# First batch of a spectral FFN kernel: biases added by VectorE while t1 leaves PSUM, and the threshold's last subtraction on GpSimd

## The chip, the core and the metric

The kernel runs on one core of one Trainium2 chip. The metric is the device time of one execution in microseconds (us), the median of the runs shown. A core has five engines that run side by side, each through its own list of instructions in a fixed order: TensorE (PE, with its weight loads PEld), VectorE (DVE), ScalarE (ACT), GpSimd (POOL) and SyncE (SP), which here issues all DMA transfers.

## The reference

A spectral layer (a transform along the sequence, a complex linear layer with biases, a soft threshold, the inverse transform) is followed by a feed-forward layer on every token. Here B = 8, S = 3008, D = 256, FF = 2048.

```python
X = np.fft.rfft(x, axis=1)
Xr, Xi = X.real, X.imag
Yr = Xr @ w_r - Xi @ w_i + b_r
Yi = Xr @ w_i + Xi @ w_r + b_i
Yr = np.sign(Yr) * np.maximum(np.abs(Yr) - 0.01, 0.0)
Yi = np.sign(Yi) * np.maximum(np.abs(Yi) - 0.01, 0.0)
y = np.fft.irfft(Yr + 1j * Yi, n=S, axis=1)
h = y.reshape(B * S, D) @ w_in
out = (h - np.tanh(h)) @ w_out
```

## The kernel before

The 8 batches go through the spectral layer one after the other, and their tokens in 48 chunks through the feed-forward layer. The spectral work of batches 1 to 7 is woven into the feed-forward work of the batch before. Batch 0 has nothing to be woven into: it runs first, by itself, and that is where the change lies. The order of the instructions on every engine is that in which the code issues them (a manual schedule); nothing reorders them later, and an instruction that waits holds up everything behind it on its engine.

Batch 0 is cut into 12 units (`WholeSpectrum(0, jp)`, called unit 0 to 11 below). The main loop runs i = 0 to 11, and pass i holds a different step of several units:

- PE: the transform of unit i into a PSUM bank (`dft`, L532); the products of unit i-1 (`cross`): a bias product of a matrix of ones with the row of biases (L551), the two cross terms into the same bank `vv` and the shared term `t1` into the bank with the tag `o0` (L557). In passes 4, 6, 8 and 10 the inverse transforms of units i-4 and i-3 follow (L612).
- ACT: copies t1 of unit i-2 out of PSUM (`common`, L573, tile `tb`), copies the transform of unit i to `xf` (L537), then for unit i-2 the two halves of the soft threshold, `up` = relu(y - 0.01) and `mn` = relu(-y - 0.01) (L586, L590), and the copies of the inverse (L623).
- DVE: adds tb and vv of unit i-2 to `y` (`blend`, L579), the sum `sf` of unit i (L542), a share of the unpacking of feed-forward weights, and last `join` of unit i-2: mn = up - mn (L603).
- The weights come as 64-bit floats and are unpacked in blocks b0, b1, ... of 128x512 numbers. A block takes five DVE steps, called e (L221), m (L236), f (L239), s (L242) and v (L245) here; two steps on ACT between e and f (L225, L232); and a rounding on ACT (L249) with the remainder on POOL (L250). In passes 2 to 4 one of three matrices of the linear layer is split as well: ACT rounds (L142), POOL, DVE, POOL subtract (L143). Table `on_dve` sets which block steps stand in which pass; in pass 8 they are f, s, v of b3 and e of b4, in pass 9 m, f, s, v of b4 and e of b5, in pass 10 m, f, s, v of b5 and e, m of b6.

`o0` is one single bank: t1 of the next unit can be written only when t1 of the last one has been read. `tb` has the tag `xi` with two buffers before. After the loop units 8 to 11 finish in code written out by hand (units 10 and 11 threshold on DVE alone, L594 and L595), batch 1's first transforms begin (L291, PE), and then the feed-forward layer.

The biases come to SBUF by one transfer before: `bias_rows`, 33 partitions. A tile `bias` on 128 partitions is loaded later for the other batches (their biases in another order of columns).

Of the kernel before, what the change touches and what calls it, by code (L numbers as in the profile page):

```python
# [92 lines left out]


@with_exitstack
def spectral_ffn(ctx, tc, x, w_r, w_i, w_in, w_out, x_fold, b_turned, f1, f1b, f1f, f2, f2f, i1, i1w, i2, out):
    nc = tc.nc
    P = 128
    w_in, w_out = w_in.bitcast(U32), w_out.bitcast(U32)
# [55 lines left out]
    def load_linear():  # L155
        wr = ffn.tile([P, 2, D], F32, name="wr_f", tag="g_h")
        wi = ffn.tile([P, 2, D], F32, name="wi_f", tag="g_l")
        nc.sync.dma_start(out=wr, in_=w_r.rearrange("(t p) e -> p t e", p=P))
        nc.sync.dma_start(out=wi, in_=w_i.rearrange("(t p) e -> p t e", p=P))
        rows = load_bias(work.tile([33, 2, D], F32, name="bias_rows", tag="tmp", bufs=4), 33)  # L160
        return wr, wi, rows

    def load_bias(dst, n):
        both = b_turned.rearrange("(o k) d -> o (k d)", o=1).to_broadcast([n, 2 * D])
        nc.sync.dma_start(out=dst.rearrange("p k d -> p (k d)"), in_=both)
        return dst

    def combine_linear(wr, wi, rows, zero):
# [4 lines left out]
        ones = work.tile([P, P], F32R, name="ones", tag="s_l")  # L173
        nc.vector.tensor_scalar(out=ones, in0=zero[:, :P], scalar1=1.0, scalar2=None, op0=ALU.add)
        top = work.tile([33, 2 * D], F32R, name="bias_top", tag="tmp", bufs=4)
        flat = rows.rearrange("o r e -> o (r e)")
        nc.scalar.copy(out=top, in_=flat)
        brow = work.tile([P, 2 * D], F32R, name="brow", tag="ot", bufs=1)
        nc.vector.tensor_copy(out=brow, in_=zero)
        nc.vector.tensor_copy(out=brow[0:1], in_=top[0:1].bitcast(F32))  # L180
        nc.vector.tensor_tensor(out=brow[32:33], in0=flat[32:33], in1=top[32:33].bitcast(F32), op=ALU.subtract)
        return (wr, w2, w3), (ones, brow)
# [333 lines left out]
    class WholeSpectrum(Spectrum):  # L516
# [27 lines left out]
        def cross(self):  # L544
            if self.jp % 3 < 2:
                self.vv = ps_h.tile([P, 512], F32, name="ps_v", tag="h")
            else:
                self.vv = ps_o.tile([P, 512], F32, name="ps_v", tag="o1")
            ones, brow = bias_rows
            by_part = self.vv.rearrange("p (r i j) -> p r i j", r=2, j=2)  # L550
            nc.tensor.matmul(by_part, ones, brow.rearrange("p (r j i) -> p r i j", r=2, j=2), start=True, stop=False)  # L551
            self.t1 = ps_o.tile([P, 512], F32, name="ps_t1", tag="o0")[:, :D]
            for k, (dst, lhs) in enumerate((
                (self.vv[:, :D], self.xf[:, :, 1]), (self.vv[:, D:], self.xf[:, :, 0]), (self.t1, self.sf),
            )):
                for t in range(2):
                    nc.tensor.matmul(dst, lhs[:, t], whole_lin[2 - k][:, t, :], start=k == 2 and t == 0, stop=k > 0 and t == 1)  # L557

        def cross_apart(self):
            ones, brow = bias_rows  # L560
# [4 lines left out]
            for dst, lhs, w, b in ((self.t1, self.sf, 0, None), (low, self.xf[:, :, 1], 2, 0), (high, self.xf[:, :, 0], 1, D)):  # L565
                if b is not None:
                    nc.tensor.matmul(paired(dst, D), ones, in_turn(brow[:, b:b + D]), start=True, stop=False)
                for t in range(2):
                    nc.tensor.matmul(dst, lhs[:, t], whole_lin[w][:, t, :], start=b is None and t == 0, stop=t == 1)

        def common(self):
            self.tb = work.tile([P, D], F32, name="tb0", tag="xi")
            nc.scalar.copy(out=self.tb, in_=self.t1)  # L573

        def blend(self):
            self.y = self.temp("y", "g")
            if not hasattr(self, "sides"):
                both = self.vv.rearrange("p (r d) -> p r d", r=2)
                nc.vector.tensor_tensor(out=self.y, in0=self.tb.unsqueeze(1).to_broadcast([P, 2, D]), in1=both, op=ALU.add)  # L579
                return  # L580
            for r, side in enumerate(self.sides):
                nc.vector.tensor_tensor(out=self.y[:, r], in0=self.tb, in1=side, op=ALU.add)

        def above(self):
            self.up = self.temp("up", "th")
# [14 lines left out]
            self.below()  # L600

        def join(self):
            nc.vector.tensor_tensor(out=self.mn, in0=self.up, in1=self.mn, op=ALU.subtract)  # L603

        def inverse(self, parts=None, banks=None, first=0):
            banks = banks or [ps_f.tile([P, 512], F32, name="ps_i1", tag="f") for _ in range(2)]
# [159 lines left out]
    with tc.manual_schedule(engines={E.PE, E.Activation, E.DVE, E.Pool, E.SP}):  # L766
# [21 lines left out]
        for i in range(len(steps) + 1):  # L788
            if i < len(steps):
                steps[i][0].whole(steps[i][1])  # L790
            if i >= 1:
# [364 lines left out]
```

## Time and profile before

| what | before |
|---|---|
| median of 3 runs | 2439.88 us (2439.38 to 2440.62) |
| the profiled execution's own time | 2442.07 us |
| span of the profiled execution | 2440.3 us |
| granted TensorE clock over the span | 1.000 |
| PE busy | 2427.9 us (99%) |
| DVE busy | 1781.2 us (73%) |
| ACT busy | 1349.6 us (55%) |
| POOL busy | 34.5 us (1%) |

The span is the time from the first to the last instruction; the profiled execution's own time is 1.8 us longer, and the runs without a profile are 2.2 us below that. The busy shares are means over the whole span: what bounds a stage has to be read in that stage. Batch 0's units lie between 26 and 87 us.

### The profile page before, as it was taken

To read this page: it belongs to the slowest core of one execution; us is meant where nothing else is said; L and a number is where in the kernel's file an instruction comes from. 1 tells how busy PE (TensorE), PEld (TensorE's weight loads), DVE (VectorE), ACT (ScalarE), POOL (GpSimd) and SP (SyncE) were. 2 spreads that over 40 slices of the span, in tenths; PEclk is the share of its full clock that TensorE was granted. 3 is DMA by queue.
4 is the path that set the end of the run, shared out by engine and by line. 5 is a ranking of instruction groups with operands and counts; after the bars stand their busy time and mean duration, and the time that the engine had idled before them with its cause. 6 is when DMAs were issued, how large, how long until landed. Compare 5 with 4: busy or idle time off the path is not lost.

```text
span 2440.3 us, 47561 instructions
## 1 busy us (share of the span) xinstructions
PE 2427.9 (99%) x19274; PEld 2134.1 (87%) x19274; DVE 1781.2 (73%) x3251; ACT 1349.6 (55%) x2781; POOL 34.5 (1%) x31
## 2 busy tenths in 40 slices
PE   9999999999999999999999999999999999999999
PEld 6798888888888898888888889888898989888888
DVE  4887887787777776777767777677776767755555
ACT  5765555555555555555555555555555555555554
POOL 2110000000000000000000000000000000000000
PEclk9999999999999999999999999999999999999999
DMA  8633216322534212332123231332211111111000
GB/s 253 193 102 111 86 65 153 91 74 81 142 88 108 76 54 67 97 98 69 61 72 100 82 94 53 81 82 80 62 61 46 59 58 43 51 34 26 21 9 17
DMA packets 135146, 195.31 MB, mean 80 GB/s; under 512 B 13521, under 2 KB 99631, under 8 KB 134928
## 3 DMA queue, kind: packets, MB, share of 16 engines
q1 hardware_dynamic: 134928, 192.29, 27.3%
q8 instruction: 151, 2.47, 0.4%
q14 instruction: 67, 0.55, 0.1%
HBM read 114.12 MB, written 78.12 MB: 79 GB/s over the span
## 4 chain that ended last, share of the span: by engine, by line
PE 93%; DVE 4%; ACT 1%; DMA 1%; issue 1%; SPq 0%; ACTq 0%; DVEq 0%
PE o L742 39%; PE h L709 38%; PE ps_v L423 4%; PE ps_i L667 3%; PE ps_t L423 2%; PE ps_f L507 2%; PE ps_f L343 1%; DVE g L723 1%; PE ps_i L479 1%; PE ps_i L480 1%; PE ps_i L478 1%; DVE gl L729 1%; PE ps_f L291 1%; DVE w_s L242 0%; DVE w_f L239 0%
## 5 line engine op out<-in xcount | busy, mean ns | idle before, releaser
L726 ACT CAST gh<-g 128x502 fp32r<-128x502 f32 (+2 forms) x768 | 469.0, 611 | 568.4 <-DVE g L723 558.6
L729 DVE TENSOR_TENSOR gl<-g,gh 128x502 fp32r<-128x502 f32 (+2 forms) x768 | 522.2, 680 | 331.9 <-ACT gh L726 322.0
L723 DVE TENSOR_TENSOR g<-h,th 128x502 f32<-128x502 f32 (+2 forms) x768 | 520.4, 678 | 218.7 <-ACT th L720 212.9
L720 ACT ACTIVATE th<-h 128x502 f32<-128x502 f32 (+2 forms) x768 | 454.1, 591 | 379.1 <-PE h L709 375.0
L742 PE MATMUL o<-gh,wout_l 128*128 128x502 f32 (+2 forms) x1536 | 587.2, 382 | 0.2 <-DVE ot L760 0.2
L742 PE MATMUL o<-gh,wout_h 128*128 128x502 f32 (+2 forms) x1536 | 576.5, 375 | 0.0
L742 PE MATMUL o<-gl,wout_h 128*128 128x502 f32 (+2 forms) x1536 | 576.1, 375 | 0.3 <-DVE gl L729 0.3
L709 PE MATMUL h<-yh,win_l 128*128 128x502 f32 (+2 forms) x1536 | 451.9, 376 | 1.4 <-DVE g L723 1.0
L709 PE MATMUL h<-yh,win_h 128*128 128x502 f32 (+2 forms) x1536 | 450.3, 375 | 0.0
L709 PE MATMUL h<-yl,win_h 128*128 128x502 f32 (+2 forms) x1536 | 450.3, 375 | 0.0
L742 PEld LDWEIGHTS o<-gh,wout_l 128*128 128x128 f32 x1536 | 290.2, 189 | 54.2 <-issue 11.7
L709 PEld LDWEIGHTS h<-yh,win_l 128*128 128x128 f32 x1536 | 288.6, 188 | 40.9 <-DVE g L723 4.6
L742 PEld LDWEIGHTS o<-gl,wout_h 128*128 128x128 f32 x1536 | 290.0, 189 | 36.2 <-DVE gl L729 1.1
L709 PEld LDWEIGHTS h<-yl,win_h 128*128 128x128 f32 x1536 | 290.4, 189 | 34.4
L709 PEld LDWEIGHTS h<-yh,win_h 128*128 128x128 f32 x1536 | 290.3, 189 | 34.4
L742 PEld LDWEIGHTS o<-gh,wout_h 128*128 128x128 f32 x1536 | 290.6, 189 | 26.4
L465 DVE TENSOR_TENSOR y<-tb,ps_v 64x256 f32<-64x256 f32 x336 | 140.0, 417 | 3.4
L700 ACT CAST yh<-yt 128x470 fp32r<-128x470 f32 (+38 forms) x200 | 90.0, 483 | 23.7 <-PE h L709 21.3
L701 DVE TENSOR_TENSOR yl<-yt,yh 128x470 fp32r<-128x470 f32 (+38 forms) x200 | 82.3, 430 | 16.6 <-ACT yh L700 15.6
L411 DVE TENSOR_TENSOR xl<-ps_f,xh 128x256 fp32r<-128x256 f32 x168 | 63.6, 419 | 27.5 <-ACT xi L409 26.0
L667 PEld LDWEIGHTS ps_i<-i,zin 48*64 48x64 f32 x4096 | 65.2, 135 | 9.5 <-issue 5.5
L142 ACT CAST z_h<-mn 128x512 fp32r<-128x512 f32 x84 | 52.5, 625 | 36.3 <-DVE mn L456 36.3
(116 smaller groups left out, 2130.4 us busy)
## 6 DMA issues: line engine op xcount, KB each, us to landing
xt<-in_x_fold SPq DMA_DIRECT2D x52, 512.0 KB
at<-a SPq DMA_DIRECT2D x96, 256.0 KB
z<-zo SPq DMA_DIRECT2D x92, 256.0 KB
zin<-z SPq DMA_DIRECT2D x92, 240.0 KB
a<-st SPq DMA_DIRECT2D x216, 96.0 KB
out<-ot SPq DMA_DIRECT2D x29, 502.0 KB
turn_l<-turns SPq DMA_DIRECT2D x72, 128.0 KB
turn_h<-turns SPq DMA_DIRECT2D x72, 128.0 KB
```

Source lines behind the costliest of these rows:

```text
L411: nc.vector.tensor_tensor(out=xl[:, s], in0=whole[s], in1=xh[:, s].bitcast(F32), op=ALU.subtract)
L423: nc.tensor.matmul(paired(dst, D), lhs[:, t], in_turn(rhs[:, t, :]), start=n == 0, stop=n == 5)
L465: nc.vector.tensor_tensor(out=self.y[ri * 64:(ri + 1) * 64, jj, :], in0=self.tb[rows, ri, :], in1=self.side(ri)[rows], op=ALU.add,)
L667: nc.tensor.matmul(pv[h][64 * c:64 * c + 64, t, 47 * k:47 * k + 47], self.zt[rows, k, at:at + 64], i2t[rows, :47], start=True, stop=True,)
L700: nc.scalar.copy(out=yh, in_=y)
L701: nc.vector.tensor_tensor(out=yl, in0=y, in1=yh.bitcast(F32), op=ALU.subtract)
L709: nc.tensor.matmul(paired(h, n), lhs[:, t, f * P:(f + 1) * P], moving(rhs[:, t], n), start=k == 0, stop=k == 5,)
L720: nc.scalar.activation(out=th[:, :n], in_=h[:, :n], func=AF.Tanh)
L723: nc.vector.tensor_tensor(out=g[:, :n], in0=h[:, :n], in1=th[:, :n], op=ALU.subtract)
L726: nc.scalar.copy(out=gh[:, :n], in_=g[:, :n])
L729: nc.vector.tensor_tensor(out=gl[:, :n], in0=g[:, :n], in1=gh[:, :n].bitcast(F32), op=ALU.subtract)
L742: nc.tensor.matmul(paired(self.o[t], n), lhs[:, f, t * P:(t + 1) * P], in_turn(rhs[:, :n]), start=f == 0 and k == 0, stop=f == NF - 1 and ...
```

## The change

For the units of batch 0, the 13 products with ones go away, and so do the tiles `ones`, `bias_top` and `brow` with the five instructions that make them. Instead the tile `bias` is loaded early (128 partitions, plain order of columns), and `common` becomes an instruction of DVE: it reads t1 from PSUM twice over, adds both biases and writes a tile of 128x512. That tile has the tag `ot` with one buffer. `blend` then reads this tile. `join` moves from DVE to POOL. The other order of the biases is loaded into the same tile later, where the load for the other batches stood.

```diff
-        rows = load_bias(work.tile([33, 2, D], F32, name="bias_rows", tag="tmp", bufs=4), 33)
-        return wr, wi, rows
+        return wr, wi
...
-            ones, brow = bias_rows
-            by_part = self.vv.rearrange("p (r i j) -> p r i j", r=2, j=2)
-            nc.tensor.matmul(by_part, ones, brow.rearrange("p (r j i) -> p r i j", r=2, j=2), start=True, stop=False)
             self.t1 = ps_o.tile([P, 512], F32, name="ps_t1", tag="o0")[:, :D]
...
         def common(self):
-            self.tb = work.tile([P, D], F32, name="tb0", tag="xi")
-            nc.scalar.copy(out=self.tb, in_=self.t1)
+            self.tb = work.tile([P, 2, D], F32, name="tb", tag="ot", bufs=1)
+            nc.vector.tensor_tensor(out=self.tb, in0=self.t1.unsqueeze(1).to_broadcast([P, 2, D]), in1=bias, op=ALU.add)
...
-                nc.vector.tensor_tensor(out=self.y, in0=self.tb.unsqueeze(1).to_broadcast([P, 2, D]), in1=both, op=ALU.add)
+                nc.vector.tensor_tensor(out=self.y, in0=self.tb, in1=both, op=ALU.add)
...
         def join(self):
-            nc.vector.tensor_tensor(out=self.mn, in0=self.up, in1=self.mn, op=ALU.subtract)
+            nc.gpsimd.tensor_tensor(out=self.mn, in0=self.up, in1=self.mn, op=ALU.subtract)
...
         bias = const.tile([P, 2, D], F32, name="bias")
+        load_bias(bias, b_plain)
         keep_warm(25)
...
-                load_bias(bias, P)
+                load_bias(bias, b_turned)
```

Two engines' lists show it. First DVE, from the end of pass 7 to the start of pass 9, before. `mn<-up,mn` is join of units 5 and 6, `y` is blend of units 6 and 7, `sf` is the sum of units 8 and 9, and the four rows between are f, s, v of block b3 and e of b4.

```order
L603 TENSOR_TENSOR mn<-up,mn 128x512
L579 TENSOR_TENSOR y<-tb_578,ps_v 128x512
L542 TENSOR_TENSOR sf<-ps_f_580,xf 128x256
L239 SCALAR_TENSOR_TENSOR w_f<-w_raw,w_m 128x512
L242 SCALAR_TENSOR_TENSOR w_s<-w_raw,w_s 128x512
L245 SCALAR_TENSOR_TENSOR w_f<-w_f,w_s 128x512
L221 TENSOR_SCALAR w_s<-w_raw 128x512
L603 TENSOR_TENSOR mn<-up,mn 128x512
L579 TENSOR_TENSOR y<-tb_640,ps_v 128x512
```

The same place of DVE's list in the changed kernel (its line numbers are 11 to 17 lower).

```order
L556 TENSOR_TENSOR tb<-ps_t_547,bias 128x512
L562 TENSOR_TENSOR y<-tb,ps_v 128x512
L531 TENSOR_TENSOR sf<-ps_f_564,xf 128x256
L228 SCALAR_TENSOR_TENSOR w_f<-w_raw,w_m 128x512
L231 SCALAR_TENSOR_TENSOR w_s<-w_raw,w_s 128x512
L234 SCALAR_TENSOR_TENSOR w_f<-w_f,w_s 128x512
L210 TENSOR_SCALAR w_s<-w_raw 128x512
L556 TENSOR_TENSOR tb<-ps_t_585,bias 128x512
L562 TENSOR_TENSOR y<-tb,ps_v 128x512
```

Where join of a unit stood, `tb` of the next unit stands now: the number of instructions is the same, and t1 is read out of PSUM only after the weight steps of the pass before. Second, POOL's list in this stage, before: the splits of two matrices and the remainders of the blocks.

```order
L172 TENSOR_TENSOR w_f<-wi_f,wr_f 128x512
L143 TENSOR_TENSOR w_l<-wr_f,w_h 128x512
L143 TENSOR_TENSOR w_l<-w_f,w_h 128x512
L250 TENSOR_TENSOR win_l<-w_f,win_h 128x512 x2
L250 TENSOR_TENSOR wout_l<-w_f,wout_h 128x512 x2
L250 TENSOR_TENSOR win_l<-w_f,win_h 128x512 x2
```

And the same stage in the changed kernel, with the ten joins between.

```order
L143 TENSOR_TENSOR w_l<-wr_f,w_h 128x512
L586 TENSOR_TENSOR mn<-up,mn 128x512 x2
L143 TENSOR_TENSOR w_l<-w_f,w_h 128x512
L586 TENSOR_TENSOR mn<-up,mn 128x512
L239 TENSOR_TENSOR win_l<-w_f,win_h 128x512
L586 TENSOR_TENSOR mn<-up,mn 128x512 x2
L239 TENSOR_TENSOR win_l<-w_f,win_h 128x512
L586 TENSOR_TENSOR mn<-up,mn 128x512
L239 TENSOR_TENSOR wout_l<-w_f,wout_h 128x512
L586 TENSOR_TENSOR mn<-up,mn 128x512
L239 TENSOR_TENSOR wout_l<-w_f,wout_h 128x512
L586 TENSOR_TENSOR mn<-up,mn 128x512
```

From pass 6 on, remainders and joins take turns on POOL.

## Rows read from the trace of the kernel before

**Rows 1.** Busy time by stretch: us, then each engine's busy us (instructions).

```profile
26.00:49.00 23.00, 21.79 (x127) 18.23 (x126) 11.18 (x19) 13.40 (x24) 1.60 (x2) 1.00 0.81 269
49.00:79.00 30.00, 29.84 (x179) 24.92 (x178) 26.68 (x44) 26.22 (x54) 9.83 (x7) 1.00 0.81 253
...
120.00:160.00 40.00, 40.00 (x203) 38.01 (x202) 39.80 (x64) 27.35 (x49) 7.79 (x6) 1.00 0.33 93
```

**Rows 2.** The chain that ended last, 26 to 93 us: start, us, what.

```profile
37.90 0.41 DVE w_m L236
...
44.22 0.60 DVE mn L603
...
62.85 0.86 PE ps_t L557 x4
63.71 1.98 PE ps_i L612 x16
```

**Rows 3.** DVE in order of time, passes 8 to 11: start, us, what [idle before].

```profile
62.99 0.69 DVE L239 SCALAR_TENSOR_TENSOR w_f<-w_raw,w_m 128x512 f32<-128x512 uint32 x1 [0.68 <-issue]
63.60 1.76 DVE L242 SCALAR_TENSOR_TENSOR w_s<-w_raw,w_s 128x512 uint32<-128x512 uint32 x1
65.39 0.69 DVE L245 SCALAR_TENSOR_TENSOR w_f<-w_f,w_s 128x512 f32<-128x512 f32 x1
...
66.34 0.68 DVE L603 TENSOR_TENSOR mn<-up,mn 128x512 f32<-128x512 f32 x1
67.18 0.69 DVE L579 TENSOR_TENSOR y<-tb,ps_v 128x512 f32<-128x512 f32 x1 [0.15 <-ACT tb L573]
...
69.09 0.69 DVE L239 SCALAR_TENSOR_TENSOR w_f<-w_raw,w_m 128x512 f32<-128x512 uint32 x1 [0.55 <-ACT w_s L232]
...
78.81 0.42 DVE L542 TENSOR_TENSOR sf<-ps_f,xf 128x256 f32<-128x256 f32 x1
79.14 0.68 DVE L579 TENSOR_TENSOR y<-tb,ps_v 128x512 f32<-128x512 f32 x1
81.23 0.69 DVE L603 TENSOR_TENSOR mn<-up,mn 128x512 f32<-128x512 f32 x1 [1.40 <-ACT mn L590]
```

**Rows 4.** PE in order of time: products of units 7 and 11.

```profile
60.66 0.46 PE L551 MATMUL ps_v<-brow,ones 128*128 128x512 f32 x1
60.96 1.89 PE L557 MATMUL ps_v<-w_f,xf 128*128 128x256 f32 x8
...
79.28 1.13 PE L569 MATMUL ps_t<-wr_f,sf 128*128 128x256 f32 x4 [0.23 <-DVE sf L542]
```

**Rows 5.** Line L447, the same addition in batches 1 to 7: ns min/median/max.

```profile
L447 DVE TENSOR_TENSOR tb<-ps_t,bias x84: 669/682/693, 237.6 to 2107.9; 128x512 f32<-128x512 f32 x84
```

**Rows 6.** POOL in order of time.

```profile
36.15 1.55 POOL L143 TENSOR_TENSOR w_l<-wr_f,w_h 128x512 fp32r<-128x512 f32 x1 [15.99 <-ACT w_h L142]
...
58.70 2.14 POOL L250 TENSOR_TENSOR win_l<-w_f,win_h 128x512 fp32r<-128x512 f32 x1 [6.97 <-ACT win_h L249]
63.49 1.32 POOL L250 TENSOR_TENSOR wout_l<-w_f,wout_h 128x512 fp32r<-128x512 f32 x1 [2.65 <-ACT wout_h L249]
...
78.35 1.67 POOL L250 TENSOR_TENSOR win_l<-w_f,win_h 128x512 fp32r<-128x512 f32 x1 [2.00 <-ACT win_h L249]
```

**Rows 7.** DVE in order of time, passes 2, 5 and 7.

```profile
36.34 1.65 DVE L221 TENSOR_SCALAR w_s<-w_raw 128x512 uint32<-128x512 uint32 x1 [2.05 <-DMA w_raw<-in_moe_w_in]
...
49.78 0.42 DVE L542 TENSOR_TENSOR sf<-ps_f,xf 128x256 f32<-128x256 f32 x1
...
59.88 1.50 DVE L603 TENSOR_TENSOR mn<-up,mn 128x512 f32<-128x512 f32 x1 [0.17 <-ACT mn L590]
```

**Rows 8.** SP's issues in order of time.

```profile
25.42 1.24 SPq L313 DMA_DIRECT2D a<-st  x2
27.74 0.64 SPq L388 DMA_DIRECT2D at<-a  x1
...
104.06 0.43 SPq L165 DMA_DIRECT2D bias<-in_b_turned  x1
```

More of the change, by code (lines that the diff above doesn't have):

```diff
@@ L95, in spectral_ffn @@
 @with_exitstack
-def spectral_ffn(ctx, tc, x, w_r, w_i, w_in, w_out, x_fold, b_turned, f1, f1b, f1f, f2, f2f, i1, i1w, i2, out):
+def spectral_ffn(ctx, tc, x, w_r, w_i, w_in, w_out, x_fold, b_plain, b_turned, f1, f1b, f1f, f2, f2f, i1, i1w, i2, out):
     nc = tc.nc
@@ L159, in load_linear, with load_bias, combine_linear @@
         nc.sync.dma_start(out=wi, in_=w_i.rearrange("(t p) e -> p t e", p=P))
-        rows = load_bias(work.tile([33, 2, D], F32, name="bias_rows", tag="tmp", bufs=4), 33)
-        return wr, wi, rows
-    def load_bias(dst, n):
-        both = b_turned.rearrange("(o k) d -> o (k d)", o=1).to_broadcast([n, 2 * D])
+        return wr, wi
+    def load_bias(dst, biases):
+        both = biases.rearrange("(o k) d -> o (k d)", o=1).to_broadcast([P, 2 * D])
         nc.sync.dma_start(out=dst.rearrange("p k d -> p (k d)"), in_=both)
-        return dst
-    def combine_linear(wr, wi, rows, zero):
+    def combine_linear(wr, wi):
         w2 = ffn.tile([P, 2, D], F32, name="w2_f", tag="g_h")
@@ L172, in combine_linear @@
         nc.gpsimd.tensor_tensor(out=w2, in0=wi, in1=wr, op=ALU.subtract)
[L173 to L182, printed above, removed]
+        return wr, w2, w3
     win_h = const.tile([P, 2, FF], F32R, name="win_h")
@@ L556, in cross @@
                 for t in range(2):
-                    nc.tensor.matmul(dst, lhs[:, t], whole_lin[2 - k][:, t, :], start=k == 2 and t == 0, stop=k > 0 and t == 1)
+                    nc.tensor.matmul(dst, lhs[:, t], whole_lin[2 - k][:, t, :], start=t == 0, stop=t == 1)
         def cross_apart(self):
-            ones, brow = bias_rows
             self.t1 = ps_f.tile([P, 512], F32, name="ps_t1", tag="f")[:, :D]
@@ L564, in cross_apart @@
             self.sides = low, high
-            for dst, lhs, w, b in ((self.t1, self.sf, 0, None), (low, self.xf[:, :, 1], 2, 0), (high, self.xf[:, :, 0], 1, D)):
-                if b is not None:
-                    nc.tensor.matmul(paired(dst, D), ones, in_turn(brow[:, b:b + D]), start=True, stop=False)
+            for dst, lhs, w in ((self.t1, self.sf, 0), (low, self.xf[:, :, 1], 2), (high, self.xf[:, :, 0], 1)):
                 for t in range(2):
-                    nc.tensor.matmul(dst, lhs[:, t], whole_lin[w][:, t, :], start=b is None and t == 0, stop=t == 1)
+                    nc.tensor.matmul(dst, lhs[:, t], whole_lin[w][:, t, :], start=t == 0, stop=t == 1)
         def common(self):
-            self.tb = work.tile([P, D], F32, name="tb0", tag="xi")
-            nc.scalar.copy(out=self.tb, in_=self.t1)
+            self.tb = work.tile([P, 2, D], F32, name="tb", tag="ot", bufs=1)
+            nc.vector.tensor_tensor(out=self.tb, in0=self.t1.unsqueeze(1).to_broadcast([P, 2, D]), in1=bias, op=ALU.add)
         def blend(self):
@@ L578, in blend @@
                 both = self.vv.rearrange("p (r d) -> p r d", r=2)
-                nc.vector.tensor_tensor(out=self.y, in0=self.tb.unsqueeze(1).to_broadcast([P, 2, D]), in1=both, op=ALU.add)
+                nc.vector.tensor_tensor(out=self.y, in0=self.tb, in1=both, op=ALU.add)
                 return
             for r, side in enumerate(self.sides):
-                nc.vector.tensor_tensor(out=self.y[:, r], in0=self.tb, in1=side, op=ALU.add)
+                nc.vector.tensor_tensor(out=self.y[:, r], in0=self.tb[:, r], in1=side, op=ALU.add)
         def above(self):
@@ L809, in spectral_ffn @@
             f.store_far()
-        whole_lin, bias_rows = combine_linear(*lin_in, zero)
+        whole_lin = combine_linear(*lin_in)
         const.tile([P, 64], F32, name="gap")
@@ L1139 @@
     given["x_fold"] = given["x_fold"].reshape(B - 1, 128, 4, 2, 2, 2 * D)
-    given["b_turned"] = np.ascontiguousarray(np.stack([given.pop("b_r"), given.pop("b_i")])[:, back], np.float32)
+    given["b_plain"] = np.stack([given.pop("b_r"), given.pop("b_i")]).astype(np.float32)
+    given["b_turned"] = np.ascontiguousarray(given["b_plain"][:, back])
     given |= dict(zip(("f1", "f1b", "f1f", "f2", "f2f", "i1", "i1w", "i2"), dft_constants()))
```

## The prediction

> **What bounds the kernel now.** I read the stretches first [rows 1]. From 49 to 79 us PE is busy 29.84 of 30 us, but DVE is at 26.68 and ACT at 26.22: three engines are near their limit at once. From 120 to 160 us DVE is busy 39.80 of 40, so what follows batch 0 starts on a full DVE and can't make up a late start. A shift of batch 0's end is therefore a shift of the kernel's end, unless something else is shown.
>
> Then the chain [rows 2]. Up to 49 us it runs through DVE and ACT (m of block b0, join of unit 1), from there through PE, where t1 takes 0.86 us and the inverses of a pair 1.98, and after 65 us through DVE. The hand-over shows on PE: t1 of unit 11 waits 0.23 us for DVE's sf at 78.81 [rows 3, 4]. So PE and DVE come out of pass 10 together, and an edit that relieves PE alone shows nothing beyond that point.
>
> Third, DVE's own rows [rows 3]. Pass 8 is f, s, v, e, join, then y and sf. A row starts 0.60 us after the one before it, for 0.69 us of duration. The waits for ACT are small: 0.15 and 0.55 us. One row stands out: s lasts 1.76 instead of 0.69 us. A POOL subtraction began at 63.49 and ended at 64.81 [rows 6]; s began at 63.60 and could do nothing until then. The same happens to e at 36.34 (1.65; m, an instruction of the same kind, takes 0.41 [rows 2]) beside POOL's 36.15, and to join at 59.88 (1.50) beside POOL's 58.70 [rows 6, 7]. Both ways: that POOL row took 2.14 us, as DVE was ahead of it. Not every DVE instruction is held: y, which reads PSUM, begins at 79.14 in the middle of POOL's row of 78.35 to 80.02 and takes its normal 0.68 [rows 3, 6]. So instructions of DVE that read only SBUF exclude POOL's and the other way round, and the second waits.
>
> **The change, part by part.**
>
> *The products with ones.* The next product starts 0.30 us behind the one with ones (60.66 to 60.96 [rows 4]). 13 of them are 3.9 us of PE. That counts only where PE is last; at the end of pass 10 it isn't, so I take 0 and keep -3.9 as the bound. The five instructions that make the row of biases run on DVE and ACT before unit 0, where these idle; 0.
>
> *tb on DVE.* The same addition, out of PSUM with the bias tile, stands 84 times in the trace: 0.682 us [rows 5]. It takes the place of join (0.68), so the count on DVE stays. But y needs tb at once, so the two can't overlap: 0.69 instead of 0.60, +0.09 a unit. ACT loses a copy per unit; ACT sets only the small waits above.
>
> *t1's bank.* t1 is in one bank. Before, ACT emptied it early; now DVE does, behind the weight steps of the pass before. PE's next t1 waits for that.
>
> *join on POOL.* 1.3 us on POOL (the row of 63.49 has the same form) in place of 0.6 on DVE. DVE saves nothing, as tb has filled its place. What join does on POOL lies beside DVE's f, s, v, e and m, which read only SBUF, or beside tb, y and sf, which read PSUM and aren't held. s lost 1.76 - 0.69 = 1.07 us to POOL; I take 1.07 for each join that meets a weight step.
>
> *The bias transfer.* It goes into SP's queue ahead of the loads for units 0 to 3, 0.43 us of issue [rows 8]. But SP idles from 26.66 to 27.74, waiting for a buffer, so the later loads, b0's raw weights among them, hardly move: +0.2; bounds 0 and +0.4. The other load of biases keeps its place.
>
> **The sum,** laid out in the new order with these durations.
>
> Passes 2 to 5, up to sf of unit 5 (49.78 before [rows 7]): the chain goes through b0's steps as before. join of unit 0 now sits on POOL right behind the split of the first matrix, and meets m: +1.07. Twice tb for join, +0.18; the transfer, +0.2. tb of unit 2 lands in the place of join of unit 1, about 45.7 instead of 44.22, and t1 of unit 3 must wait until 46.3; behind it stand t1's 0.86, both inverses (1.98) and the transform of unit 5 with its copy on ACT (some 2 us more), so sf of unit 5 comes at about 51.2. Both ways give +1.4.
>
> Passes 5 to 10, up to sf of unit 11 (78.81): in pass 5 POOL's list holds the last split, join, remainder and join in a row, and s and e of DVE meet two of them: +2.14. In pass 6 join meets s: +1.07. In pass 7 join falls beside tb and y, and the stall of 59.88 shrinks by 0.4. In passes 8, 9 and 10 s meets the remainder as before, and then v meets join, which POOL starts as soon as s has let go: 3 x 1.07 = +3.2. Six times tb: +0.5. The ACT waits of 0.15 and 0.55 are covered by then: -0.7. Together 2.14 + 1.07 - 0.4 + 3.2 + 0.5 - 0.7 = +5.8.
>
> Tail, units 9 to 11: DVE no longer waits 1.40 for `mn` of unit 9 and does no join (-2.0), but adds tb of units 10 and 11 (+1.4), and the threshold of unit 10 meets the last join on POOL (+0.9); dependent pairs +0.2. Together +0.5.
>
> 1.4 + 5.8 + 0.5 = +7.7 us. The profiled execution's span of 2440.3 becomes 2448.0, its own time, 1.8 above that, 2449.8; the median of the runs, 2439.88, becomes **2447.6 us**.
>
> The Trainium skill has a rule for this (SBUF — State Buffer, Who interferes with whom): the pair of ports that DVE and GpSimd share is an exclusive lock, and a DVE instruction with two SBUF inputs, or one in a two-port mode, blocks fully against a GpSimd instruction that reads SBUF, for the whole of that instruction. The trace agrees in kind; in size the rows show 1.07 lost beside a POOL row of 1.32. By the rule each of the eight meetings would cost up to 0.25 more, some 2 us in all, and the time would be about 2449.6.
>
> **The rivals.**
>
> *Joins find the gaps.* POOL may come to the ports only when DVE turns to tb, y and sf, 1.5 us without an SBUF-only instruction in each pass. For it speaks POOL's row of 58.70: two DVE instructions passed in front of it, and it took 2.14 us. Against it: beside 63.49 POOL got in between f and s, though DVE ran them back to back. Place: v in passes 8 to 10, s in passes 5 and 6. The eight meetings drop out (-8.4), the ACT waits come back (+0.7), and PE's wait for t1's bank remains; about +1, 2441 us, no measurable change. It decides once more than three of the eight joins find a gap (7.7 - 3 x 1.07 = 4.5). This is the case on the other side.
>
> *The time is given back after batch 0.* The feed-forward steps after 87 us also wait for transfers; if these were last, some of the +7.7 would vanish. Against it: DVE at 39.80 of 40. If half is absorbed, +3.8: 2443.7.
>
> *PE is the bound after all.* Then the 3.9 us of products come off and nothing else counts: 2436.0. Against it: PE's wait at 79.28 and the new wait for t1's bank.
>
> **How the numbers follow.** What a measurement of this kernel can tell from no change is about 0.2%, 4.9 us. Forecast (+4.5 to +11): 0.66. Joins in gaps: 0.18. Given back: 0.08. PE bound: 0.08. Nearly all of the first is slower by over 0.2%, a little of the second and third as well: slower 0.66, same 0.31, faster 0.03, as even all 3.9 us of PE stay within 0.2%. The range reaches down to the case of the gaps, 2440.5, leaving out the last case, and up to the rule's 2449.6 with two more meetings, 2451.5. The likeliest case's own range is 2444.4 to 2451.
>
> **What would show it.** Right: s and v of passes 8 to 10 both at about 1.7 us; t1 of unit 3 waiting for tb on DVE by 2 us or more; sf of unit 11 at about 86; weight steps beside a join longer than 1 us in six to eight places. Wrong: POOL's joins with 2 us or more themselves while DVE's rows stay at 0.69 (the gaps); PE without idle time up to 76 us (PE bound); sf of unit 11 late by 7 us and the kernel's end not (given back). The forecast fails most easily in the number of meetings, which hangs on a few tenths of a microsecond in when ACT's `mn` ends.

## The result, and the profile after

The changed kernel takes 2452.99 us (median of 4 runs, 2451.72 to 2454.55), the kernel before 2440.1 us beside it (4 runs, 2439.38 to 2440.62). The ratio is 1.0052, with a 95% interval of 1.004 to 1.0065: slower, by 12.9 us where 7.7 were forecast, and outside the range. The profiled execution of the changed kernel took 2454.55 us, with a span of 2452.8 us against 2440.3.

First the loss is put in its place. The first product of batch 1 on PE ends batch 0; this is its line in the kernel before, by instruction: duration in ns as min/median/max, then first and last start in us.

```profile
L291 PE MATMUL ps_f<-xt,f1b_f x16: 589/592/697, 86.7 to 97.6; 94*128 94x512 f32 x16
```

And the same line in the changed kernel (all its line numbers here are 11 to 17 lower than before).

```profile
L280 PE MATMUL ps_f<-xt,f1b_f x16: 592/592/697, 100.0 to 110.0; 94*128 94x512 f32 x16
```

13.2 us are lost by the first of these products (99.96 against 86.72 us, rounded in these lines) and 12.5 at the end of the span: the loss lies in batch 0, and nothing to speak of is given back. The stretches of the changed kernel answer to [rows 1]; the columns after the busy times are the granted clock, the DMA share and GB/s.

```profile
26.00:49.00 23.00, 17.77 (x94) 14.80 (x96) 13.17 (x21) 10.27 (x15) 4.21 (x3) 0.93 0.76 260
49.00:79.00 30.00, 26.59 (x147) 21.41 (x144) 21.47 (x29) 19.44 (x38) 13.91 (x9) 0.88 0.55 182
...
120.00:160.00 40.00, 39.74 (x201) 37.48 (x200) 39.58 (x65) 28.78 (x51) 6.41 (x5) 1.00 0.43 134
```

From 49 to 79 us every engine but POOL is less busy than before: PE 26.59 instead of 29.84 us, DVE 21.47 instead of 26.68. A stage in which all engines idle more is held by a chain between them. And the clock is 0.93 and 0.88 where it was 1.00. Finer windows of the changed kernel show where it fell.

```profile
26.00:44.00 18.00, 14.71 (x84) 12.73 (x84) 8.24 (x11) 8.94 (x13) 4.21 (x3) 1.00 0.82 279
...
46.00:48.00 2.00, 2.00 (x6) 1.17 (x6) 2.00 (x5) 1.30 (x2) 0.00 (x0) 0.50 0.26 92
48.00:49.00 1.00, 1.00 (x6) 0.83 (x8) 0.96 (x3) 0.03 (x1) 0.00 (x0) 0.50 0.00 0
...
50.00:58.00 8.00, 6.93 (x42) 5.71 (x40) 3.13 (x4) 6.25 (x12) 5.05 (x4) 1.00 0.64 195
...
60.00:66.00 6.00, 5.66 (x20) 3.72 (x20) 5.79 (x9) 2.22 (x4) 1.76 (x1) 0.50 0.14 49
...
67.00:79.00 12.00, 12.00 (x73) 10.17 (x72) 10.01 (x14) 9.56 (x20) 6.03 (x4) 1.00 0.72 245
```

In two stretches the granted clock is 0.50, that is 1.2 GHz instead of 2.4. PE in order of time shows what stood before each: the bracket is PE's idle time and what ended it.

```profile
45.94 2.05 PE L543 MATMUL ps_t<-wr_f,sf 128*128 128x256 f32 x4 [2.35 <-DVE tb L556]
47.92 2.71 PE L595 MATMUL ps_i<-mn,turns 64*128 64x256 f32 x16
50.56 1.16 PE L521 MATMUL ps_f<-f,at 128*128 128x128 f32 x8
...
60.34 2.07 PE L543 MATMUL ps_t<-wr_f,sf 128*128 128x256 f32 x4 [3.41 <-DVE tb L556]
62.34 3.79 PE L595 MATMUL ps_i<-mn,turns 64*128 64x256 f32 x16
66.05 1.34 PE L521 MATMUL ps_f<-f,at 128*128 128x128 f32 x8
...
84.53 1.13 PE L543 MATMUL ps_t<-wr_f,sf 128*128 128x256 f32 x4 [2.75 <-DVE tb L556]
85.59 2.00 PE L595 MATMUL ps_i<-mn,turns 64*128 64x256 f32 x16
87.52 1.16 PE L521 MATMUL ps_f<-f,at 128*128 128x128 f32 x8
```

The three rows with brackets are t1 of units 3, 5 and 9, each waiting for `tb` to empty the one bank. The third time the clock holds: from t1 to the next transform 2.99 us pass (84.53 to 87.52). The first time the same steps take 4.62 us (45.94 to 50.56), the second time 5.71 (60.34 to 66.05): 1.6 and 2.7 us more. t1 takes 2.05 instead of 1.13 us there and the inverses up to 3.79 instead of 2.00; before, the chain had 0.86 and 1.98 for them [rows 2]. The Trainium skill (TensorE: Matmul & The Clock Gate, HAM oscillation — how this bites in real kernels) describes a PE that waits for data, is throttled to half its clock, and starts the next tile's products cold. Its example waits for a DMA; here the trace shows the same behind a wait for VectorE.

DVE does in passes 8 to 10 what was forecast. In order of time, where [rows 3] has s at 1.76 and v at 0.69 us:

```profile
73.60 1.76 DVE L231 SCALAR_TENSOR_TENSOR w_s<-w_raw,w_s 128x512 uint32<-128x512 uint32 x1
75.39 1.64 DVE L234 SCALAR_TENSOR_TENSOR w_f<-w_f,w_s 128x512 f32<-128x512 f32 x1
...
86.61 1.76 DVE L231 SCALAR_TENSOR_TENSOR w_s<-w_raw,w_s 128x512 uint32<-128x512 uint32 x1
88.40 1.65 DVE L234 SCALAR_TENSOR_TENSOR w_f<-w_f,w_s 128x512 f32<-128x512 f32 x1
...
91.24 0.41 DVE L531 TENSOR_TENSOR sf<-ps_f,xf 128x256 f32<-128x256 f32 x1
```

And POOL beside the first pair, a remainder and then join, as in [rows 6]:

```profile
73.47 1.34 POOL L239 TENSOR_TENSOR wout_l<-w_f,wout_h 128x512 fp32r<-128x512 f32 x1 [1.84 <-PE ps_t L543]
74.77 1.72 POOL L586 TENSOR_TENSOR mn<-up,mn 128x512 f32<-128x512 f32 x1
```

v now loses 0.95 us (1.64 - 0.69) to join, as s loses 1.07 to the remainder. So two things cost time in this profile: the ports, as forecast, and a clock that the forecast did not have in it.

### The profile page after: what moved, and what is told of

It is laid out like the page before. It is cut to its first block, busy times and chain, and to the rows that moved or that the text cites. A ratio compares the mean times of both kernels' runs of the same rounds, so it can differ in the third digit from the quotient of the medians.

```text
span 2452.8 us, 47522 instructions
## 1 busy us (share of the span) xinstructions
PE 2428.6 (99%) x19261; PEld 2134.3 (87%) x19261; DVE 1790.4 (73%) x3249; ACT 1345.9 (55%) x2768; POOL 49.7 (2%) x41
## 4 chain that ended last, share of the span: by engine, by line
PE 93%; DVE 4%; ACT 1%; issue 1%; DMA 1%; SPq 0%; ACTq 0%; DVEq 0%
PE o L725 39%; PE h L692 38%; PE ps_v L412 4%; PE ps_i L650 3%; PE ps_t L412 2%; PE ps_f L496 2%; PE ps_f L332 1%; DVE g L706 1%; PE ps_f L280 1%; PE ps_i L469 1%; PE ps_i L468 1%; PE ps_i L467 1%; DVE gl L712 1%; DVE w_s L231 1%; PE ps_i L595 0%
## 5 line engine op out<-in xcount | busy, mean ns | idle before, releaser
L396 ACT CAST xh<-ps_f 128x256 fp32r<-128x256 f32 x168 | 54.0, 373 | 33.5 <-DVE xi L402 33.5
```

## The experiments

The table has all runs in one measure, beside the times. Batch 0 on the chain is measured from the start of m of block b0 on DVE, where the chain of [rows 2] begins (37.90 us before), to the first product of batch 1 (86.72 before): 48.82 us before. The start of m itself moves by up to 3 us from kernel to kernel, with the landing of the raw weights, and is left out this way. One thing crosses this line: POOL's first join holds up either m (1.5 us instead of 0.4), and then its 1.1 us are in the measure, or e just ahead of m, and then they aren't. In the changed kernel, e1, e2, e5 and e6 it is m; in e7, e9, e10 and e12 it is e. "Third transform" is the distance that the expectations name, from PE's third transform to the same first product; it includes PE's slack ahead of m, and the measure from m is the better one. "Span" is the profiled execution's span less the 2440.3 us of before. The kernel before had a median of 2439.76 to 2440.55 us in these jobs.

| kernel | median us (range, runs) | ratio [95% interval] | from m us | against before | third transform us | span |
|---|---|---|---|---|---|---|
| before | 2440.1 | | 48.82 | | 54.57 | |
| changed | 2452.99 (2451.72 to 2454.55, 4) | 1.0052 [1.004, 1.0065] | 62.27 | +13.4 | 68.07 | +12.5 |
| e1_fill | 2455.1 (2452.35 to 2455.53, 5) | 1.0055 [1.0042, 1.0068] | 59.46 | +10.6 | 65.26 | +13.4 |
| e2_join_only | 2443.38 (2442.38 to 2444.66, 11) | 1.0011 [1.0003, 1.002] | 50.78 | +2.0 | 56.53 | +0.3 |
| e3_bias_only | 2451.12 (2449.47 to 2454.62, 5) | 1.0044 [1.003, 1.0058] | 57.52 | +8.7 | 63.32 | +9.1 |
| e4_no_products | 2439.97 (2438.68 to 2441.03, 11) | 0.9997 [0.9988, 1.0006] | 48.41 | -0.4 | 54.37 | -3.4 |
| e5_two_banks | 2450.04 (2448.87 to 2450.56, 5) | 1.0039 [1.0026, 1.0052] | 55.70 | +6.9 | 61.50 | +8.0 |
| e6_fill_more | 2451.58 (2450.24 to 2452.78, 5) | 1.0045 [1.0032, 1.0059] | 58.90 | +10.1 | 64.69 | +9.5 |
| e7_bias_late | 2450.84 (2449.99 to 2454.09, 5) | 1.0045 [1.0033, 1.0058] | 58.23 | +9.4 | 65.25 | +8.7 |
| e8_rest_on_dve | 2439.65 (2438.02 to 2444.07, 11) | 1.0 [0.9991, 1.0009] | 47.79 | -1.0 | 53.54 | -4.1 |
| e9_fill_all | 2452.93 (2452.83 to 2453.47, 5) | 1.0051 [1.0037, 1.0065] | 56.73 | +7.9 | 63.76 | +11.2 |
| e10_two_banks_fill | 2447.37 (2445.83 to 2450.5, 8) | 1.0028 [1.0018, 1.0038] | 53.73 | +4.9 | 60.76 | +3.7 |
| e11_two_banks_dve_join | 2447.72 (2445.48 to 2453.85, 5) | 1.0036 [1.0023, 1.005] | 54.73 | +5.9 | 61.24 | +4.3 |
| e12_fill_less | 2451.26 (2450.55 to 2452.74, 5) | 1.0048 [1.0035, 1.0061] | 56.76 | +7.9 | 63.78 | +10.6 |

The two theories after the result: (A) the ports and t1's bank cost what was forecast, and the rest is PE at half clock behind its new waits; (B) the ports or the bank cost more than forecast, and the clock is a side effect.

**Each part alone.** The kernel before with join on GpSimd, and nothing else:

```diff
-            nc.vector.tensor_tensor(out=self.mn, in0=self.up, in1=self.mn, op=ALU.subtract)
+            nc.gpsimd.tensor_tensor(out=self.mn, in0=self.up, in1=self.mn, op=ALU.subtract)
```

> The kernel before with join alone moved to GpSimd; biases by products with ones, t1 copied by ACT. By the trace of the changed kernel, where v of passes 8 to 10 takes 1.65 us beside a join, ports alone should cost here: DVE loses 0.6 us of join a pass but some 1.0 at each meeting; the sum is +2 to +3.5 us, 2442 to 2443.5, with TensorE at full clock, since t1's bank is emptied early by ACT. Rival (the joins are the main cost, the bias part nearly free): +8 us or more, 2448. Rival (joins find gaps): -1 to 0, 2439.

Measured: +2.0 us, and the time 1.0011 times that of before. DVE's v beside a join, and the join, in order of time:

```profile
64.58 1.65 DVE L245 SCALAR_TENSOR_TENSOR w_f<-w_f,w_s 128x512 f32<-128x512 f32 x1
```

```profile
63.96 1.72 POOL L603 TENSOR_TENSOR mn<-up,mn 128x512 f32<-128x512 f32 x1
```

So joins meet weight steps even where DVE has a step of 0.6 us less in each unit, and what they take there is more than what DVE saves. The clock stays at 1.00. The other part, the changed kernel with join back on VectorE (the edit above, turned round):

> The changed kernel with join back on VectorE: only the biases' part of the change. Theory A (t1's one bank is emptied late by DVE, TensorE waits, its clock falls): TensorE waits for tb by 2 us or more in several passes, DVE has 0.69 us more a unit, and the time is +6 us without and +9 to +11 us with a fall of the clock: 2446 to 2451. Rival (the joins are the main cost): within 2 us of before, 2440 to 2442.

Measured: +8.7 us, with one stretch of half clock (47.5 to 51.5 us) behind a wait of 2.87 us for tb. Both parts lose by themselves. The third part is the products with ones: the kernel before without them, which leaves the biases of batch 0 out.

```diff
-            nc.tensor.matmul(by_part, ones, brow.rearrange("p (r j i) -> p r i j", r=2, j=2), start=True, stop=False)
...
-                if b is not None:
-                    nc.tensor.matmul(paired(dst, D), ones, in_turn(brow[:, b:b + D]), start=True, stop=False)
```

> The kernel before without the 13 products with ones and nothing in their place: this run leaves the biases of batch 0 out. It prices what the change removes. My sum took 0, with -3.9 us as the bound: PE and DVE come out of pass 10 together, so -0.3 to -1 us, 2439 to 2440. If TensorE is the bound of this stage: -3.9 us, 2436.

Measured: -0.4 us from m, and a ratio of 0.9997: 13 products less on PE are worth nothing that can be told, though PE looks full there.

**Keeping the clock up.** If half clock is the missing term, work that keeps PE going through the waits should bring it back. The changed kernel, with products of zeros added into the sum of `vv` ahead of t1 of some units, so many for each unit (they add zero):

```diff
+                    if k == t == 1:
+                        for _ in range(FILL.get(self.jp, 0)):
+                            nc.tensor.matmul(dst, hush, hush.unsqueeze(1).to_broadcast([P, 2, P]), start=False, stop=False)
...
+        hush = work.tile([P, P], F32R, name="hush", tag="s_l")
+        nc.vector.tensor_copy(out=hush, in_=zero[:, :P])
+        FILL = {1: 8, 2: 12, 4: 17, 8: 14}
```

> The changed kernel, with products of a tile of zeros added to the second cross term of units 1, 2, 4 and 8 (8, 12, 17 and 14 of them, 256 columns), so that TensorE has work where it now waits for tb. The sums don't change. Theory A (half the miss is TensorE's clock: after its waits of 2.35 and 3.41 us for tb the granted clock is 0.50 until 49 and 66 us): the clock stays at 1.00, t1 of units 3 and 5 take 1.1 us instead of 2.0, the inverses behind them 2.0 instead of 2.7 and 3.8, and the time falls by 4 to 5 us to about 2448. Theory B (the clock is a by-product, the chain runs through DVE and the shared ports anyway): 2452 to 2454, no change beyond 1 us. If the fillers are longer than the waits, they cost up to 1 us.

Measured: +10.6 us from m, but a time that is no better, which settles nothing by itself. t1 of unit 5 kept its clock, and from sf of unit 5 to sf of unit 11 the loss is +6.0 us instead of the changed kernel's +8.8. But half clock at t1 of unit 3 stayed (48.8 to 53 us), and a new one came at the very start, as PE in order of time shows:

```profile
29.16 3.50 PE L521 MATMUL ps_f<-f,at 128*128 128x128 f32 x16 [3.04 <-issue]
```

Two transforms take 3.50 us at half clock, behind 3.04 us of idle time; m started at 40.89 us, 3.0 later than before. The bias load stands ahead of the first loads on SP's queue. In the next two kernels it goes behind the first three:

```diff
         bias = const.tile([P, 2, D], F32, name="bias")
-        load_bias(bias, b_plain)
...
+        load_bias(bias, b_plain)
```

The changed kernel with this edit alone:

> The changed kernel with the biases' load moved in SP's queue behind the loads of units 0 to 2. It prices the transfer that I took at +0.2 us. In the run with fillers the first transform came at 29.16 after 3.04 us of idle TensorE, at half clock; in the changed kernel at 26.72 after 1.22 us; in the kernel before at 26.58 after 0.15 us. If the transfer delays the first transform: -0.5 to -2 us, 2451 to 2452.5, and single runs closer together than 2451.7 to 2454.6. If the delay has another cause: no change, 2453.

Measured: +9.4 us instead of +13.4, and PE's first transform waits 0.18 us. But the 4.0 us are not the bias load: 1.1 of them are the join that meets e here and not m, and most of the rest is the clock, as PE's rows show:

```profile
44.55 1.13 PE L543 MATMUL ps_t<-wr_f,sf 128*128 128x256 f32 x4 [2.35 <-DVE tb L556]
45.61 2.00 PE L595 MATMUL ps_i<-mn,turns 64*128 64x256 f32 x16
47.54 1.16 PE L521 MATMUL ps_f<-f,at 128*128 128x128 f32 x8
...
57.34 2.08 PE L543 MATMUL ps_t<-wr_f,sf 128*128 128x256 f32 x4 [3.44 <-DVE tb L556]
59.35 2.60 PE L595 MATMUL ps_i<-mn,turns 64*128 64x256 f32 x16
```

The same t1 with the same wait of 2.35 us, which was followed by half clock in the changed kernel, keeps full clock here: t1 1.13 and the inverses 2.00 us. With the wait unchanged and the clock not, the steps from t1 to the transform take 2.99 instead of 4.62 us. That is the clock's price by itself.

The same late bias load with zeros before t1 of units 1, 2 and 4 (FILL 8, 24, 20):

> As the run with fillers, with two corrections from its trace: there the wait in front of t1 of unit 3 was still 1.92 us idle and the clock was at 0.50 from about 48 to 52, and the first transform came 2.4 us later than in the changed kernel. Now 24 products of zeros in unit 2's sum, 20 in unit 4's and 8 in unit 1's, and the biases are loaded behind the loads of units 0 to 2. The sums don't change. Theory A: clock 1.00 from 30 to 70 us, sf of unit 5 within 2 us of its time in the kernel before (counted from the first transform), and the time at 2447 to 2449. Rival (clock is a by-product): 2452 to 2455.

Measured: +10.1 us. The clock is 1.00 up to 79 us, and m meets a join as in the changed kernel: up to sf of unit 5 (37.02 to 51.12 us) the loss is +2.2 us, against the changed kernel's +3.8 with half clock. Then half clock moved on to t1 of unit 9 (79 to 85.5 us, behind a wait of 2.75 us): 5.72 us from t1 to the transform instead of 2.99. Of these 2.7 us, 1.1 arrive at sf of unit 11 (from sf of unit 5 to there 36.05 us, against 35.00 in the next kernel); without them it is +9.0. With zeros before units 1, 2, 4 and 8 (FILL 8, 20, 20, 14):

> The changed kernel with the biases' load behind the loads of units 0 to 2 and products of zeros before t1 in units 1, 2, 4 and 8 (8, 20, 20, 14). The sums don't change. In the second run with fillers the one fall of the clock left (0.50 from about 79 to 85 us) came after a wait of 2.75 us for tb in unit 9, and stretched the way from that t1 to the next transform from 3.0 to 5.7 us. Theory A (ports, DVE's longer passes and the late emptying cost some 7 us, the falls of the clock the rest): no fall between 30 and 80 us, from the third transform to the first product of batch 1 62 us (54.6 before, 68.1 in the changed kernel), time 2447 to 2449. Rival (something else costs the rest): 2451 or more with the clock at 1.00.

The stretches of this kernel:

```profile
26.00:50.00 24.00, 22.87 (x148) 20.23 (x147) 12.23 (x21) 12.84 (x21) 4.18 (x4) 1.00 0.77 259
50.00:79.00 29.00, 26.78 (x170) 22.96 (x169) 26.31 (x34) 20.35 (x38) 17.09 (x11) 1.00 0.75 231
79.00:104.00 25.00, 22.82 (x259) 15.50 (x258) 21.81 (x36) 15.26 (x32) 8.51 (x6) 1.00 0.46 130
```

Now the clock is 1.00 throughout, PE's waits for tb are at most 1.2 us, and batch 0 costs +7.9 us from m instead of +13.4. Not all of these 5.5 us are the clock's. This is m of b0 in the changed kernel, beside POOL's first join:

```profile
37.69 1.49 DVE L225 TENSOR_SCALAR w_m<-w_raw 128x512 uint32<-128x512 uint32 x1
```

And here, where that join held up e (1.06 us instead of 0.42), ahead of the measure:

```profile
37.28 0.41 DVE L225 TENSOR_SCALAR w_m<-w_raw 128x512 uint32<-128x512 uint32 x1
```

That is 1.1 us. The other 4.4 are the clock's, and with m's meeting the change costs +9.0 us at full clock, as e6_fill_more gives it too: theory A in kind, with more than its 7 us for the rest. Yet the median was no better than that of the changed kernel: from the first product (+7.3) to the end (+11.2) 3.9 us were lost again. 3.0 of them lie in the transforms of a later batch: at 595 us the addition `tb` of the woven work comes 6.8 us later than before, and at 708 us 9.8 us later. SP's issues there, in order of time: the store of a tile of results to memory, then its reading back, and the load of x behind it.

```profile
605.89 0.52 SPq L479 DMA_DIRECT2D z<-zo  x1
610.56 0.32 SPq L641 DMA_DIRECT2D zin<-z  x1
610.94 0.44 SPq L317 DMA_DIRECT2D xt<-in_x_fold  x1
```

From store to reading back 4.67 us pass, against 2.53 before (599.11 to 601.64). The load of x waits behind it in the queue, and DVE, in order, waits for x:

```profile
614.86 1.29 DVE L323 TENSOR_TENSOR e<-xt 128x512 f32<-128x512 f32 x2 [2.42 <-DMA xt<-in_x_fold]
...
633.56 1.29 DVE L323 TENSOR_TENSOR e<-xt 128x512 f32<-128x512 f32 x2 [2.58 <-DMA xt<-in_x_fold]
```

Before, these waits are 0.65 and 0.97 us. Whether that was an accident was asked with two products of zeros less before t1 of unit 8 (FILL 8, 20, 20, 12):

> The kernel with zero products before t1 of units 1, 2, 4 and 8 and the bias load behind the first loads, with 12 instead of 14 zero products before t1 of unit 8: all else is the same. In the run with 14, the read of z at 610 us waited 4.1 us for the store of z (2.0 in the kernel before and in the changed one), the x load queued behind it on SyncE came late, VectorE waited 2.42 and 2.58 us for x, and 3.9 us were lost after batch 0. Theory A (an accident of how that store met other transfers, moved by any small shift): the read of z waits about 2 us again, VectorE's waits for x are below 1.1 us, the span from the first product of batch 1 to the end is that of the kernel before (2353.5 us) within 1 us, and the time is 2448 to 2450.5 us. Theory B (a lasting cost of the zero products or of the later bias load): the wait is again about 4 us and the time 2452 to 2454 us.

Measured: +7.9 us from m again, at a clock of 1.00, so the measure of batch 0 repeats. But the time is 2451.26 us: the reading back came 4.01 us after the store (605.91 to 609.92), and DVE waited 1.76 and 3.45 us for x. So it is no accident of one execution. The DMA view of e9_fill_all from 605 to 611 us has one thing that the changed kernel's view of the same store lacks, a load of instructions:

```profile
GB/s 0 0 0 0 0 0 55 116 123 300 328 260 314 219 225 464 355 328 314 96 0 0 0 0 0 0 14 0 14 14 14 27 14 14 0 0 0 0 0 0
...
q1 hardware_dynamic: 432, 0.52, 27.2%
q8 instruction: 1, 0.02, 1.7%
```

The row GB/s cuts the 6 us into 40 slices: the store's last packets trickle in at 14 GB/s after a pause. e12_fill_less shows the same load and the same trickle. But in e6_fill_more such a load lies near the store too, and the reading back followed after 2.65 us. That the load of instructions holds up the store is therefore not shown; why the store was late stays open. For batch 0 it doesn't matter.

**Taking the wait away.** The changed kernel with t1 in two banks in turn (`vv` then always has the tag h):

```diff
-            if self.jp % 3 < 2:
-                self.vv = ps_h.tile([P, 512], F32, name="ps_v", tag="h")
-            else:
-                self.vv = ps_o.tile([P, 512], F32, name="ps_v", tag="o1")
-            self.t1 = ps_o.tile([P, 512], F32, name="ps_t1", tag="o0")[:, :D]
+            self.vv = ps_h.tile([P, 512], F32, name="ps_v", tag="h")
+            self.t1 = ps_o.tile([P, 512], F32, name="ps_t1", tag=f"o{self.jp % 2}")[:, :D]
```

> The changed kernel with t1 on two banks in turn (o0 and o1) and the cross terms on the two banks of tag h alone, so that TensorE's next t1 needn't wait until DVE has read the last one. Theory A (late emptying of t1's bank makes TensorE idle, its clock falls, and the half-speed rows behind it delay the inverses and transforms that DVE waits for): waits for tb go, TensorE's idle time is cut into pieces of mostly 0.7 to 2 us, the clock stays at 1.00 from 30 to 78 us, and the time falls by 4 to 6 us, to 2447 to 2449. Rival (the chain runs through DVE and the ports whatever TensorE does): no more than 1 us, 2452.

Measured: +6.9 us, and a time of 2450.04 us, 1 us above theory A's range. The waits for tb are gone, and the clock is 1.00 up to 82 us. Then PE waits for the sum of unit 11 instead, and pays once, 1.0 us (from sf of unit 11 to the first product +1.6 us, against +0.6 in the next kernel); without it +5.9:

```profile
84.37 2.07 PE L549 MATMUL ps_t<-wr_f,sf 128*128 128x256 f32 x4 [3.52 <-DVE sf L531]
86.23 3.62 PE L549 MATMUL ps_v<-w_f,xf 128*128 128x256 f32 x8
```

With the late bias load and 16 zeros before t1 of unit 10 as well:

> The changed kernel with t1 on two banks in turn, the biases' load behind the loads of units 0 to 2, and 16 products of zeros before t1 of unit 10, where the run with two banks had its only fall of the clock (0.50 from about 83.5 to 88.5 us, after a wait of 3.52 us for sf of unit 11; two products 3.62 instead of 1.89 us). Theory A: clock 1.00 from 30 to 90 us, from the third transform to the first product of batch 1 60 to 61 us, time 2446 to 2447.5: what is left is DVE's longer passes and its meetings with POOL. Rival: 2449 or more with the clock at 1.00.

```profile
26.00:49.00 23.00, 22.01 (x132) 18.98 (x131) 12.58 (x21) 12.70 (x21) 4.28 (x4) 1.00 0.81 271
49.00:79.00 30.00, 27.51 (x165) 22.46 (x165) 27.83 (x38) 22.53 (x44) 19.19 (x12) 1.00 0.79 233
79.00:104.00 25.00, 21.76 (x245) 14.36 (x244) 21.50 (x36) 14.81 (x31) 7.06 (x6) 1.00 0.48 137
```

Measured: +4.9 us at a clock of 1.00, and 1.0028 times the time of before. DVE is at 27.83 of 30 us from 49 to 79, above the 26.68 of [rows 1]: with PE's waits and the half clock taken away, DVE is what is left. m meets no join here, as the first join held up e (1.43 us); with that meeting the change stands at the +5.9 of the run before. The last question was how much of that is join on POOL. The same kernel with join on VectorE:

> The kernel with t1 in two banks, the zero products before t1 of unit 10 and the bias load behind the first loads, with join back on VectorE: of the change only the bias addition by VectorE and the missing products remain, at an undisturbed clock. It splits the +6.2 us that the same kernel with join on GpSimd showed from the third transform to the first product of batch 1 (60.76 against 54.57 before). Theory A (GpSimd's joins hold VectorE up at the shared SBUF ports, and moving them off VectorE saves nothing): the distance shrinks to 57 to 59 us, and the time to 2443 to 2445.5 us. Theory B (the joins cost nothing net, since VectorE is full and would spend the same time on them itself; the additions out of PSUM are the cost): distance 60 to 62 us, time 2446.5 to 2448.5 us.

Measured: +5.9 us, of which 0.9 belong to a last stretch of half clock that this kernel has and the other has not:

```profile
89.19 2.04 PE L595 MATMUL ps_i<-mn,turn 64*128 64x256 f32 x8 [1.51 <-issue]
```

2.04 us, against 1.14 for the same eight products in e10_two_banks_fill. So +5.0 with join on VectorE, and with join on POOL +4.9 without the first join's meeting or +5.9 with it: theory B of this run. Where DVE also has tb, the joins on POOL cost at least as much in blocked steps as they save in DVE's list; the medians (2447.72 and 2447.37 us) can't tell the two apart. What costs is the addition out of PSUM on DVE; what vv on two banks and the zero products add to the 5.0 was not tested apart.

**Back to the ports.** The same balance, in the kernel before: the remainders of the blocks, which block DVE's s there [rows 3, 6], taken from POOL to VectorE (one of the passes is shown).

```diff
-            nc.gpsimd.tensor_tensor(out=lo, in0=self.w, in1=hi.bitcast(F32), op=ALU.subtract)
+        def rest(self):
+            hi, lo = places(*self.at)
+            nc.vector.tensor_tensor(out=lo, in0=self.w, in1=hi.bitcast(F32), op=ALU.subtract)
...
-            7: [b2.value, b3.mantissa],
+            7: [b2.value, b3.mantissa, b1.rest],
```

> The kernel before, with the opposite move: the blocks' remainders (16 subtractions, 0.60 us of DVE each) go from GpSimd to VectorE, behind the weight steps of the same pass. Ports theory: DVE loses 1.07 us to a remainder of POOL where it meets a weight step (passes 8, 9, 10 and one before), and some 0.85 us in each of eight steps from 100 to 160 us (e at 1.28 instead of 0.42), so doing the subtraction itself for 0.60 is cheaper: -0.5 us up to the end of batch 0 and -1 to -2 us behind it, 2437.5 to 2439. Rival (meetings cost nothing where ACT or PE is last): +2 to +5 us, as DVE gets 9.6 us more work.

Measured: a ratio of 1.0, -1.0 us from m: no change that can be told. No version of the change, and none of its parts, beats the kernel before.

## Why the prediction was wrong in size

The prediction's sum has three parts, each with its own milestones: m of b0, sf of unit 5, sf of unit 11, the first product. The table sets it beside the changed kernel and beside the same parts at a clock of 1.00. For passes 2 to 5 these are from e6_fill_more, as m meets a join there as in the changed kernel; the rest is from e9_fill_all. Each number is the stretch's length less that of the kernel before: 11.88 (37.90 to 49.78), 29.03 (49.78 to 78.81) and 7.91 us (78.81 to 86.72).

| part | forecast | clock 1.00 | changed kernel |
|---|---|---|---|
| passes 2 to 5 | +1.2 (1.4 less the 0.2 of the transfer) | +2.2 (37.02 to 51.12) | +3.8 (37.69 to 53.39) |
| passes 5 to 10 | +5.8 | +6.0 (50.28 to 85.28) | +8.8 (53.39 to 91.24) |
| tail | +0.5 | +0.8 (85.28 to 94.01) | +0.8 (91.24 to 99.96) |
| sum | +7.5 | +9.0 | +13.4 |

The step that failed is in the first two parts: "behind it stand t1's 0.86, both inverses (1.98) and the transform". The durations were read from a PE that had not waited, and set behind a wait that the forecast itself had made ("t1 of unit 3 waiting for tb on DVE by 2 us or more", measured 2.35). PE came out of that wait, and of the next like it (3.41 us, t1 of unit 5, which the forecast didn't have), at half clock. The missing term is 1.6 us in passes 2 to 5 (3.8 - 2.2) and 2.8 in passes 5 to 10 (8.8 - 6.0), 4.4 us in all, and it stands in PE's rows: 4.62 and 5.71 instead of 2.99 us, 1.6 and 2.7 more. Without it the time would be some 2448.6 us by this estimate, inside the range.

The 1.5 us between +7.5 and +9.0 are of the same step for the most part. From the transform of unit 5 to its sf "some 2 us more" were taken; it took 2.83 (50.56 to 53.39), as ACT has the four copies of the inverse (1.20) and the rounding of a matrix (1.15) ahead of the copy to xf. With 2.99 instead of 0.86 + 1.98 ahead of it that makes 1.0 us. That e9_fill_all, with +7.9, comes within 0.4 us of the forecast is luck: it has these 1.0 us, and lacks the 1.07 of m's meeting, which the forecast had counted.

The other steps:

- **Products with ones, 0 (bound -3.9).** Right: -0.4 us in e4_no_products, a ratio of 0.9997.
- **tb on DVE.** The duration was right: 674/677/690 ns against the 682 of [rows 5]. The words "the count on DVE stays" hold, but e11 shows what that hides: with join kept on DVE, tb costs 5.0 us, the missing products set off.
- **t1's bank.** The wait was named, and its length was right. PE's later waits (3.41, 2.75) were left out. Two banks take 3.0 us off at full clock (+4.9 instead of +7.9, m without a join in both). Of these 1.1 lie in passes 2 to 5, where the forecast had counted the wait. 1.1 lie in pass 6, where with two banks a join finds a gap: POOL's row at 58.32 takes 2.13 us and e 0.45, against 1.49 for e at 60.02 in e9_fill_all. The remaining 0.8 were not traced. So no run shows that the later waits cost much but for the clock behind them.
- **Joins, 1.07 for each of eight meetings.** Right in kind, nearly in number: seven of the ten joins meet a DVE step (m, e twice, v three times, the threshold of unit 10), for 0.94 to 1.07 us each (threshold 1.37 - 0.43, m 1.49 - 0.42). The 0.25 us more for each that the prediction worked out from the Trainium skill's rule (SBUF — State Buffer, Who interferes with whom) isn't there. The rule itself agrees with the rows: v at 75.39 ends 0.54 us after POOL's join beside it (77.03 against 76.49), so it did wait to the end of that row. But it came up when the row had begun, and lost less than the row's length.
- **The bias transfer, 0 to +0.4.** On the chain it was 0 in the changed kernel (the raw weights' first step at 36.28 against 36.34 us), but the bound may have been too narrow: in e1_fill, with the same transfer in the same place, m came 3.0 us late. PE's first transform waited 1.22 and 3.04 us in these two kernels, and 0.18 where the load stands behind three others (e7_bias_late). How much of the 3.0 us is the transfer's was not shown.
- **Rival "joins find the gaps"**: no, v is at 1.63 to 1.65 us; with two banks one join did. **"Given back after batch 0"**: no, +13.2 at the first product and +12.5 at the end. **"PE the bound"**: no, e4_no_products. None of the rivals had the clock in it, and so the range ended 1.5 us below the time.

## What to carry to other kernels

A wait that an edit puts on TensorE can cost more than its length: price the products that follow it at both clocks as bounds (here 4.4 of 13.4 us came that way). Moving an evacuation of a single PSUM bank to a fuller engine makes such a wait; a second bank takes it away, but not the load on the engine. And an instruction moved to GpSimd to free VectorE is worth only what it doesn't block there: here it gained nothing.

## What was not expected of the hardware

- The same wait does not always lower the clock: 2.35 us ahead of t1 of unit 3 were followed by a clock of 0.50 in the changed kernel and of 1.00 in e7_bias_late; 2.75 us ahead of t1 of unit 9 by 1.00 in the changed kernel and 0.50 in e6_fill_more.
- A store's completion can be 1.5 to 2.1 us later (4.01 and 4.67 instead of 2.53 us) 500 us behind the only place that was edited, and take back some 3 us of what the edit had gained. This was seen in two kernels (e9_fill_all, e12_fill_less), and its cause is open.
